# A gated recurrence and a multiplicative feed-forward on one core: the first 512 tokens handled by token halves, the last tile in two strips, and a new written order

## The chip, the cores and the metric

The kernel runs on one core of a Trainium2 chip. Its five engines work from queues of their own and meet at semaphores: TensorE (PE) multiplies matrices into PSUM, VectorE (DVE), ScalarE (ACT) and GpSimd (POOL) work elementwise, and SyncE (SP) issues the loads and stores, which the core's DMA engines carry out. The metric is the time of one execution on the device in microseconds (us); lower is better.

## The reference

There are 4 sequences of 5824 tokens with 256 channels, 23296 tokens in all. First comes a gated linear recurrence along each sequence, channel by channel:

```
log_a = 8 * sigmoid(r) * log(clip(sigmoid(a_param)))
a     = exp(log_a)
u     = sqrt(max(1 - a*a, 1e-6)) * sigmoid(i) * x
h[t]  = a[t] * h[t-1] + u[t]          # y = h
```

Then each token's y goes through a feed-forward with a product in place of an activation, with weights w1 and w2 (256 x 1024), w3 (1024 x 1024) and w_out (1024 x 256):

```
out = (((y @ w1) * (y @ w2)) @ w3) @ w_out
```

Inputs and output are float32.

## The kernel before

**Tiling.** Tokens go in chunks `c`: two of 256, then 44 of 512, then one of 256. The gates of chunks 0 and 1 are computed together, as one tile of 512 tokens that belongs to chunk 0 (`gates_of`). Each chunk passes through a line of steps, each with a letter in the written order:

- `r`, `i`, `x`: loads (L145). `R`: tanh of r (L157 where the tile is turned on PE, else L159). `V`: turn from tokens on partitions to channels on partitions, on PE against an identity (L197, for the chunks in `TURN_R`) or by a DMA (L208). `d`: the decay a = exp(scale * tanh + scale) (L220), one instruction for each half of 128 channels. `s`: its square (ACT L228, else L230). `q`: sqrt(1 - square) (L235).
- `I`: tanh of i (L165). `p`: plus one (L170, POOL). `t`: times x (L189 on POOL, two halves; L186 on DVE for chunk 0, with the plus one in it). `U`: the turn of this product u, on PE (L197, chunks in `TURN_U`) or by DMA.
- `g`: root times u (L245 or L248). `h`: the scan along time (L266), one for each channel half, starting from the chunk before. `y`: its cast to bf16 (L278).
- `a` and `b`: up products with w1 and w2 (L289). The 1024 hidden channels are four pairs of 128; `a` does one half pair into a PSUM tile of its own, `b` a whole pair. `c` copies `a`'s result to SBUF (ACT L305 or DVE L303, by the set `DV_COPY`). `m` multiplies the copy with `b`'s PSUM tile (L317, DVE).
- `D`: down product of 128 tokens (L331): 8 matmuls of 256 columns against a weight that is w3 @ w_out, folded once. `e` copies two such tiles out of PSUM, `o` stores them (L351). The last chunk has its own copies and stores, one for each 128 tokens (`evac_last`, `store_last`, L347).

**The fold.** The weights come in 512 KB pieces (`L..`), are cast to bf16 (`C..`: POOL L387, ACT L385 or DVE, by `W_ACT` and `W_DVE`), and each of w3's 8 row blocks is turned on PE (`Ft` L392), copied (`Fc`), multiplied with w_out (`Fm` L403) and scaled by 0.25 into the folded weight (`Fe`; ACT or DVE by `FOLD_ACT`). No `D` can run before the last `Fe`.

**Constants.** `A0` to `A2` compute the log-decay of each channel from `a_param` by a chain of tiny DVE instructions on 128x2 tiles.

**What sets the order.** The steps' order is written out as one string, `ORDER`, of 2457 words; each word emits its instructions, and every engine takes its own in that order and no other. `W` emits two matmuls on the identity whose result nobody reads. PSUM has two rings here: four buffers (`po`) shared by `a`, the turns, the fold and `D`, and two (`pb`) for `b` and `W`: the `b` two further on waits for the product `m` that reads the same buffer. Up to eight loads are under way at a time; the next is issued when an earlier one has landed.

Of the kernel before, what the change touches and what calls it, by code (L numbers as in the profile page):

```python
# [18 lines left out]
LOG1P = (2.00000001, 0.66666316, 0.40024854, 0.27961419, 0.28174657)  # L19
# [3 lines left out]
def kernel(  # L23
# [57 lines left out]
    TURN_U = {0, 2, 3, 4, 5, 6, 7}  # L81
# [3 lines left out]
    DV_SQUARE = {(0, 1), (11, 0)}  # L85
    AC_SQUARE = {(2, 0), (2, 1), (3, 0), (3, 1), (4, 0), (4, 1), (5, 0), (7, 0), (8, 0), (10, 0), (11, 1), (12, 0),
        (14, 0), (14, 1), (15, 0), (15, 1)}
    DV_CAST = set()
    AC_CAST = set()
    DV_COPY = {(0, 0, 0), (0, 0, 1), (0, 1, 0), (0, 1, 1), (0, 2, 0), (1, 0, 0), (1, 0, 1), (1, 1, 0), (1, 1, 1), (1,  # L90
        3, 0), (2, 0, 1), (2, 1, 0), (2, 1, 1), (2, 2, 0), (2, 3, 0), (2, 3, 1), (3, 0, 0), (3, 1, 0), (3, 2, 1), (3,
        3, 0), (4, 0, 0), (4, 0, 1), (4, 1, 1), (4, 2, 0), (4, 2, 1), (5, 1, 1), (5, 3, 0), (5, 3, 1), (6, 0, 0), (6,
        0, 1), (6, 2, 0), (6, 3, 1), (7, 0, 0), (7, 2, 0), (7, 3, 0), (7, 3, 1), (8, 3, 0), (10, 0, 1), (10, 1, 0),
        (10, 1, 1)}
    DV_EVAC = {(2, 0), (8, 0), (8, 1), (9, 0), (9, 1)}
    FOLD_ACT = {('c', 7), ('e', 3), ('e', 4)}
    W_ACT = {('w1', 1), ('w2', 0), ('w3', 0)}
    W_DVE = set()
# [3 lines left out]
    WARM = [2] * 16  # L102
    RINGS = {"r": 4, "i": 5, "x": 4, "th_r": 3, "u": 2, "rt": 2, "ut": 6, "a": 6, "nrm": 6, "h": 2, "y": 4,
# [38 lines left out]
    def load(c, nm):  # L142
        n = width(c) // P
        t = ring(loads, [P, 4, D], F32, name=nm + "_t", tag=nm)
        nc.sync.dma_start(  # L145
            out=t[:, :n, :],
            in_=src[nm][starts[c]:starts[c] + width(c), :].rearrange("(p n) c -> p n c" if long_rows(c) else "(n p) c -> p n c", p=P))
        T[nm, c] = t

    def tanh_r(c, half=None):  # L150
# [4 lines left out]
        if c in TURN_R:  # L155
            cols = slice(None) if half is None else slice(half * P, half * P + P)
            nc.scalar.activation(out=flat(t)[:, :n, cols], in_=T["r", c][:, :n, cols], func=AF.Tanh, scale=0.5)  # L157
        else:
            nc.scalar.activation(out=dense(t, n).rearrange("p cb j q -> p j cb q"), in_=cut(T["r", c])[:, :n],  # L159
                                 func=AF.Tanh, scale=0.5)  # L160
# [30 lines left out]
    def turn_pe(c, key, nm, half=None):  # L191
        n = width(c) // P
        cbs = range(NCB) if half is None else (half,)
        pt = ring(psum_o, [P, len(cbs), CT], BF16, name="ptr", tag="po")
        for cb in cbs:
            for j in range(n):
                nc.tensor.matmul(  # L197
                    out=pt[:, cb - cbs[0], j * P:(j + 1) * P],
                    lhsT=flat(T[nm, c])[:, j, cb * P:(cb + 1) * P], rhs=ident,
                    is_transpose=True,  # L200
                    start=(cb == cbs[0] and j == 0), stop=(cb == cbs[-1] and j == n - 1))
        T[(key, c) if half is None else (key, c, half)] = pt
# [9 lines left out]
    def decay(c, cb):  # L212
# [4 lines left out]
        pr = T["pr", c, cb][:, 0, :w] if ("pr", c, cb) in T else T["pr", c][:, cb, :w]  # L217
# [33 lines left out]
    def scan(c, cb):  # L251
        w = sizes[c]
        first = ("h", c) not in T
        if first:
            T["h", c] = ring(ypool, [P, NCB, CT], F32, name="h_t", tag="h")
        h = T["h", c][:, :, :w]
# [6 lines left out]
        if starts[c] % S != 0:  # L263
            pw = sizes[c - 1]
            init = T["h", c - 1][:, cb, pw - 1:pw]
        nc.vector.tensor_tensor_scan(h[:, cb, :], a[:, cb, :], n[:, cb, :], init, ALU.mult, ALU.add)  # L266

    def cast(c, cb=None):
        w = sizes[c]
        if ("y", c) not in T:  # L270
            T["y", c] = ring(ypool, [P, NCB, CT], BF16, name="y_t", tag="y")
        key = c if cb is None else (c, cb)
        cbs = slice(None) if cb is None else cb
        y, h = T["y", c][:, cbs, :w], T["h", c][:, cbs, :w]
# [11 lines left out]
    def up(c, m, dst, w_sb):  # L286
        w = sizes[c]
        for cb in range(NCB):
            nc.tensor.matmul(out=dst[:, :w], lhsT=w_sb[:, cb, m * P:(m + 1) * P],  # L289
                             rhs=T["y", c][:, cb, :w], start=(cb == 0), stop=(cb == NCB - 1))  # L290

    def up_a(c, mp, q):
        T["pa", c, mp, q] = pp = ring(psum_o, [P, CT], F32, name="pa", tag="po")
        up(c, 2 * mp + q, pp, w1_sb)

    def up_b(c, mp):
        T["pb", c, mp] = pp = ring(psum_b, [P, 2, CT], F32, name="pb", tag="pb")
        for q in range(2):
            up(c, 2 * mp + q, pp[:, q, :], w2_sb)
# [7 lines left out]
    def copy(c, mp, q):  # L307
        w = sizes[c]
        if ("sa", c, mp) not in T:
            T["sa", c, mp] = ring(ffn, [P, 2, CT], BF16, name="sa", tag="sa")  # L310
        copy_to((c, mp, q) in DV_COPY, T["sa", c, mp][:, q, :w], T["pa", c, mp, q][:, :w])

    def product(c, mp):
        w = sizes[c]
        if ("g", c) not in T:
            T["g", c] = ring(ffn, [P, KD, CT], BF16, name="g_t", tag="g")
        nc.vector.tensor_mul(out=T["g", c][:, 2 * mp:2 * mp + 2, :w], in0=T["sa", c, mp][:, :, :w],  # L317
                             in1=T["pb", c, mp][:, :, :w])

    def pair(c, j2):  # L320
        return min(2, sizes[c] // P - 2 * j2)

    def down(c, j):
        if c == NCH - 1:
# [309 lines left out]
```

## Time and profile before

The median of three executions is 511.82 us (511.63 to 512.12).

| | us |
|---|---|
| the profiled execution | 511.82 |
| its span, first to last instruction | 510.0 |
| PE busy | 502.2 (98%) |
| ACT busy | 463.3 (91%) |
| DVE busy | 429.8 (84%) |
| POOL busy | 318.2 (62%) |
| r of chunk 0 issued, landed | 0.74, 4.37 |
| first up product (chunk 0) | 13.30 |
| first up product of chunk 2 | 26.16 |
| last matmul group of the last chunk, copied out from | 506.90 |

A line of the profile names the line of the kernel, the engine, the operation and the tiles, written one first, with shapes; in the timeline the first two numbers are start and length, `xN` is how many instructions follow each other, and the bracket says how long the engine had stood and what released it. Lengths of neighbours on an engine overlap a little, so the distance between two starts tells better than a length what an instruction costs its queue. Matmuls are pipelined: a group of 128x512 matmuls starts one every 0.216 us, of 128x256 every 0.109 us, though each is shown longer.

### The profile page before, as it was taken

How to read it: one execution, taken by the hardware profiler on the slowest of the kernel's cores; microseconds unless marked ns; L12 is line 12 of the kernel's file. 1: busy time of each engine (PE TensorE's matmuls, PEld its weight loads, DVE VectorE, ACT ScalarE, POOL GpSimd, SP SyncE). 2: the span in 40 equal slices, each digit the busy share in tenths (PEclk: the TensorE clock that was granted, in tenths of full speed). 3: DMA queues.
4: the chain of work that ended last, by engine and by line, in shares of the span. 5: the costliest groups of instructions: out<-in, count | busy, mean ns of one | idle time of the engine just before them, and what ended most of it. 6: DMA issues, size and time to landing. Idle time of an engine off the chain costs nothing.

```text
span 510.0 us, 8879 instructions
## 1 busy us (share of the span) xinstructions
PE 502.2 (98%) x3217; PEld 308.2 (60%) x3217; DVE 429.8 (84%) x417; ACT 463.3 (91%) x711; POOL 318.2 (62%) x274
## 2 busy tenths in 40 slices
PE   7999999999999999999999999999999999999997
PEld 3777655665565656556666556565566655656566
DVE  5999999999999789878879799878877797959762
ACT  7999999998999999999999999998998979888543
POOL 3775878557558936965786973956647568580200
PEclk9999999999999999999999999999999999999999
DMA  8999999999989997896999996898786895252313
GB/s 319 407 413 307 379 275 276 304 302 257 309 232 282 303 282 248 191 322 184 256 306 317 262 285 163 233 245 227 206 250 151 231 319 149 91 164 64 66 48 105
DMA packets 177904, 124.06 MB, mean 243 GB/s; under 512 B 87362, under 2 KB 173892, under 8 KB 177860
## 3 DMA queue, kind: packets, MB, share of 16 engines
q1 hardware_dynamic: 177856, 123.50, 85.2%
q8 instruction: 25, 0.41, 0.3%
q14 instruction: 19, 0.16, 0.1%
q10 hardware_dynamic: 4, 0.00, 0.0%
HBM read 78.91 MB, written 23.86 MB: 201 GB/s over the span
## 4 chain that ended last, share of the span: by engine, by line
PE 90%; ACT 4%; DVE 2%; issue 2%; DMA 1%; DVEq 0%; ACTq 0%
PE po L331 30%; PE pb L289 29%; PE pa L289 28%; PE pw L403 1%; ACT sa L305 1%; PE ptr L197 1%; DVE g_t L317 1%; DMA r_t<-in_r_gate_dram 1%; PE ptw L392 1%; DVE sa L303 1%; DVE h_t L266 1%; ACT L165 1%; ACT L235 1%; ACT nrm L235 0%; ACT i_t L165 0%
## 5 line engine op out<-in xcount | busy, mean ns | idle before, releaser
L317 DVE TENSOR_TENSOR g_t<-sa,pb 128x1024 bf16<-128x1024 bf16 (+1 forms) x188 | 218.6, 1180 | 60.6 <-PE pb L289 29.0
L289 PEld LDWEIGHTS <-w_sb 128*128 128x128 bf16 x1504 | 146.5, 98 | 144.0 <-issue 3.4
L305 ACT CAST sa<-pa 128x512 bf16<-128x512 f32 (+1 forms) x336 | 180.9, 588 | 27.7 <-PE pa L289 17.6
L289 PE MATMUL pa<-y_t,w_sb 128*128 128x512 bf16 (+1 forms) x752 | 190.6, 372 | 0.4 <-ACT sa L305 0.2
L289 PE MATMUL pb<-y_t,w_sb 128*128 128x512 bf16 (+1 forms) x752 | 185.2, 372 | 0.6 <-DVE g_t L317 0.6
L331 PE MATMUL po<-wp_sb,g_t 128*128 128x256 bf16 x1456 | 178.0, 273 | 0.0
L331 PEld LDWEIGHTS <-g_t 128*128 128x128 bf16 x1456 | 142.4, 98 | 40.6 <-issue 0.5
L278 POOL CAST y_t<-h_t 128x1024 bf16<-128x1024 f32 (+2 forms) x49 | 52.5, 1074 | 146.0 <-DVE h_t L266 142.2
L189 POOL TENSOR_TENSOR u_t<-i_t,x_t 128x512 bf16<-128x512 f32 (+1 forms) x90 | 122.2, 1374 | 4.1 <-issue 2.0
L266 DVE TENSOR_TENSOR_SCAN h_t<-a_t,h_t,nrm 128x512 f32<-128x512 f32 (+1 forms) x92 | 120.8, 1343 | 1.6
L230 POOL TENSOR_TENSOR nrm<-a_t 128x512 f32<-128x512 f32 x74 | 83.0, 1139 | 12.9 <-ACT a_t L220 10.1
L220 ACT ACTIVATE a_t<-rt,la 128x512 f32<-128x512 bf16 (+1 forms) x82 | 66.0, 823 | 0.0
L305 ACT COPY ot<-po 128x512 f32<-128x512 f32 x86 | 50.5, 591 | 12.0 <-PE po L331 11.8
L248 DVE SCALAR_TENSOR_TENSOR nrm<-nrm,ut 128x1024 f32<-128x1024 f32 (+1 forms) x39 | 53.3, 1368 | 5.8 <-ACT nrm L235 5.8
L170 POOL TENSOR_SCALAR i_t<-i_t 128x1024 f32<-128x1024 f32 (+1 forms) x44 | 52.9, 1204 | 7.9 <-ACT i_t L165 7.9
L165 ACT ACTIVATE i_t<-i_t 128x1024 f32<-128x1024 f32 (+1 forms) x46 | 48.9, 1064 | 0.1
L235 ACT ACTIVATE nrm<-nrm 128x1024 f32<-128x1024 f32 (+1 forms) x47 | 48.3, 1041 | 0.2
L159 ACT ACTIVATE th_r<-r_t 128x1024 bf16<-128x1024 f32 (+1 forms) x41 | 43.5, 1060 | 0.0
L303 DVE CAST sa<-pa 128x512 bf16<-128x512 f32 (+1 forms) x40 | 23.4, 615 | 0.6 <-PE pa L289 0.5
L235 ACT ACT_TABLE_LOAD x17 | 21.8, 1283 | 0.3
L165 ACT ACT_TABLE_LOAD x9 | 11.5, 1283 | 0.2
L283 PE MATMUL warm<-ident 128*128 128x512 bf16 x32 | 10.1, 457 | 0.0
(55 smaller groups left out, 119.3 us busy)
## 6 DMA issues: line engine op xcount, KB each, us to landing
r_t<-in_r_gate_dram SPq DMA_DIRECT2D x45, 512.0 KB, 5.3
i_t<-in_i_gate_dram SPq DMA_DIRECT2D x45, 512.0 KB, 5.6
x_t<-in_x_dram SPq DMA_DIRECT2D x45, 512.0 KB, 5.5
out_dram<-ot SPq DMA_DIRECT2D x90, 256.0 KB, 3.3
wf<-in_moe_w_dram SPq DMA_DIRECT2D x12, 512.0 KB, 10.5
wf<-in_moe_w_out_dram SPq DMA_DIRECT2D x2, 512.0 KB, 10.6
rt<-th_r SPq DMA_TRANSPOSE x41, 4.4
ut<-u_t SPq DMA_TRANSPOSE x39, 4.1
```

The source lines that it names most:

```text
L165: nc.scalar.activation(out=t[:, :n, :], in_=t[:, :n, :], func=AF.Tanh, scale=0.5)
L170: (nc.vector if c in DV_PLUS else nc.gpsimd).tensor_scalar(t, t, 1.0, 1.0, op0=ALU.add, op1=ALU.mult)
L189: (nc.vector if (c, half) in DV_HALF else nc.gpsimd).tensor_mul(out=u, in0=t, in1=xt)
L220: nc.scalar.activation(out=a, in_=pr, func=AF.Exp, scale=la4[:, cb:cb + 1], bias=la4[:, cb:cb + 1])
L230: (nc.vector if (c, cb) in DV_SQUARE else nc.gpsimd).tensor_mul(out=n, in0=a, in1=a)
L235: nc.scalar.activation(out=n, in_=n, func=AF.Sqrt, scale=-1.0, bias=1.0)
L248: nc.vector.scalar_tensor_tensor(out=n, in0=n, scalar=1e-3, in1=T["pu", c][:, :, cols], op0=ALU.max, op1=ALU.mult)
L266: nc.vector.tensor_tensor_scan(h[:, cb, :], a[:, cb, :], n[:, cb, :], init, ALU.mult, ALU.add)
L289: nc.tensor.matmul(out=dst[:, :w], lhsT=w_sb[:, cb, m * P:(m + 1) * P], rhs=T["y", c][:, cb, :w], start=(cb == 0), stop=(cb == NCB - 1))
L305: nc.scalar.copy(out=dst, in_=src_ps)
L317: nc.vector.tensor_mul(out=T["g", c][:, 2 * mp:2 * mp + 2, :w], in0=T["sa", c, mp][:, :, :w], in1=T["pb", c, mp][:, :, :w])
L331: nc.tensor.matmul(out=po, lhsT=T["g", c][:, k, j * P:(j + 1) * P], rhs=wp_sb[:, k, :], start=(k == 0), stop=(k == KD - 1), skip_group_che ...
```

## The change

- r of chunk 0 (512 tokens) is loaded in two DMAs of 256 KB, each with half of the tokens; tanh and the turn on PE go by the same halves. Before, load and tile were whole, and tanh and turn went by channel halves. A decay instruction (128 channels, all 512 tokens) now reads both turned halves.
- For chunks 0 and 1 the first two of four pairs of up products are done on 256 tokens each, with both `a` halves in one PSUM tile, so that one copy serves both; the last two pairs are done once on 512 tokens. h, y and g of the two chunks share one tile, and the down product runs over them as one chunk.
- The down product of the last 128 tokens is done in two strips of 128 output channels, each with its copy (first DVE, then ACT) and its store.
- Chunk 9's u is turned on PE, no longer by a DMA.
- The chain of constants is one DVE instruction shorter.
- The sets that assign squares, casts, copies and evacuations to engines are new: six of `Fe` and `Fc` are on ACT, for three; of the weight casts ACT has two, for three, and DVE one; chunk 1's y is cast on DVE and ACT.
- The written order has 2442 words. It is new up to about chunk 14; its last 1607 words are those of before. In the new order w1's first piece is loaded ahead of i and x of chunk 0, and w3's piece 2 ahead of x of chunk 2. Of the 32 `W` matmuls, 4 stand ahead of the turns of r, 10 between them and the turn of u, 12 between that and the first up product, and 6 behind; before it was 4, 6, 16 and 6.

```diff
+LOG1P = tuple(c / 2 ** (2 * k + 1) for k, c in
+              enumerate((2.00000001, 0.66666316, 0.40024854, 0.27961419, 0.28174657)))
...
-    TURN_U = {0, 2, 3, 4, 5, 6, 7}
+    TURN_U = {0, 2, 3, 4, 5, 6, 7, 9}
...
-    FOLD_ACT = {('c', 7), ('e', 3), ('e', 4)}
-    W_ACT = {('w1', 1), ('w2', 0), ('w3', 0)}
-    W_DVE = set()
+    FOLD_ACT = {('c', 3), ('c', 7), ('e', 4), ('e', 5), ('e', 6), ('e', 7)}
+    W_ACT = {('w1', 1), ('w3', 0)}
+    W_DVE = {('w3', 5)}
...
+    HALVED = 2
...
-    def load(c, nm):
+    def load(c, nm, half=None):
         n = width(c) // P
+        js = slice(0, n) if half is None else slice(half * n // 2, (half + 1) * n // 2)
...
+        nc.sync.dma_start(out=T[nm, c][:, js, :], in_=rows[:, js, :])
...
-            cols = slice(None) if half is None else slice(half * P, half * P + P)
-            nc.scalar.activation(out=flat(t)[:, :n, cols], in_=T["r", c][:, :n, cols], func=AF.Tanh, scale=0.5)
+            js = slice(0, n) if half is None else slice(half * n // 2, (half + 1) * n // 2)
+            nc.scalar.activation(out=flat(t)[:, js, :], in_=T["r", c][:, js, :], func=AF.Tanh, scale=0.5)
...
+        js = range(n) if half is None else range(half * n // 2, (half + 1) * n // 2)
+        for cb in range(NCB):
+            for j in js:
...
+    def in_half(c, mp):
+        return c < 2 and mp < HALVED
+
+    def span(c, mp):
+        return part(c) if in_half(c, mp) else slice(0, width(c))
...
     def up_a(c, mp, q):
+        if in_half(c, mp):
+            if ("pa", c, mp) not in T:
+                T["pa", c, mp] = ring(psum_o, [P, 2, sizes[c]], F32, name="pa", tag="po")
+            up(c, mp, q, T["pa", c, mp][:, q, :], w1_sb)
+            return
...
+    def strips(c, j):
+        whole = not (c == NCH - 1 and j == sizes[c] // P - 1)
+        return [slice(0, D)] if whole else [slice(0, P), slice(P, D)]
...
     def store_last(c, j):
         t0 = starts[c] + j * P
-        nc.sync.dma_start(out=out[t0:t0 + P, :], in_=T["ot", c, j // 2][:, j % 2, :])
+        for cols in strips(c, j):
+            nc.sync.dma_start(out=out[t0:t0 + P, cols], in_=T["ot", c, j // 2][:, j % 2, cols])
...
     ORDER = """
-        r0 i0 x0 A3. E A0. A1. A2. R0.1 R0.0 W7 W10 V0.1 V0.0 W3 W14 W4 d0.1 s0.1 d0.0 s0.0 I0 q0.0 t0.0 t0.1 U0 g0
-        h0.0 W1 W2 W12 W5 W13 W8 W0 W15 h0.1 q0.1 g1 h1.1 h1.0 Lw1.0 Cw1.0 y0.1 y0.0 i2 Lw2.0 I2 r2 Lw1.1 Cw2.0 a0.0.1
...
+        r0.1 r0.0 Lw1.0 i0 x0 Lw2.0 i2 r2 Lw1.1 Lw3.2 x2 Lwo.1 Lwo.0 Lw2.1 r4 A3. E A0. A1. A2. R0.1 W6 W10 V0.1 R0.0
+        V0.0 d0.1 s0.1 d0.0 s0.0 I0 q0.0 t0.1 t0.0 W0 W14 W5 W3 W1 U0 W13 W12 W7 W15 W8 W9 g0 h0.0 h0.1 Cw1.0 Cw2.0
+        q0.1 I2 R2 y0.0 y0.1 a0.0.1 a0.0.0 W11 b0.0 V2 Cw3.2 g1 h1.0 h1.1 y1.0 Cw1.1 y1.1 d2.1 d2.0 s2.1 s2.0 q2 W2
+        a0.1.0 a1.0.1 a0.1.1 a1.0.0 c0.0.0 m0.0 b1.0 c1.0.0 m1.0 c0.1.0 a1.1.0 a1.1.1 W4 c1.1.0 b0.1 Ft2 Fc2 m0.1 p2
+        t2.0 t2.1 b1.1 U2 a0.2.0 a0.3.0 a0.2.1 Cwo.0 Cwo.1 Cw2.1 g2 m1.1 h2.0 h2.1 r3 R4 c0.2.0 c0.2.1 c0.3.0 R3
...
```

## The prediction

> **What bounds the kernel now.** I read the page's busy times first, then the chain that ended last, then the stretches, then the timeline of the first 30 us and of the last five.
>
> ```profile
> PE 502.2 (98%) x3217; PEld 308.2 (60%) x3217; DVE 429.8 (84%) x417; ACT 463.3 (91%) x711; POOL 318.2 (62%) x274
> PE 90%; ACT 4%; DVE 2%; issue 2%; DMA 1%; DVEq 0%; ACTq 0%
> ```
>
> PE is busy for 98% of the span and is 90% of the chain. The stretches tell where the rest is.
>
> ```profile
> 13.30:26.16 12.86, 12.47 (x119) 9.75 (x118) 12.74 (x25) 12.80 (x20) 9.68 (x11) 1.00 1.04 409
> 26.16:115.00 88.84, 88.79 (x628) 56.87 (x626) 85.94 (x98) 88.11 (x124) 61.87 (x56) 1.00 1.10 322
> 115.00:124.00 9.00, 8.42 (x48) 4.54 (x47) 8.70 (x9) 7.43 (x12) 7.42 (x5) 1.00 0.85 243
> 124.00:510.00 386.00, 382.59 (x2386) 232.94 (x2384) 314.78 (x264) 344.80 (x546) 235.16 (x194) 1.00 0.80 217
> ```
>
> The columns are length, then busy time of PE, PEld, DVE, ACT, POOL, then clock, DMA share, GB/s. From 26.16 to 115 us PE has 0.05 us without work, but ACT (0.73 us idle) and DVE (2.9 us) are nearly as full, and the DMA engines are saturated. So before 115 us four resources end together; after it PE alone. Any PE instruction added costs its full time, and only idle PE time can be won. There is little after 26.16: 0.58 us before one `pb` group at 122.8, and some tenths. The 1.5 us by which the first stretch exceeds its work (64 up matmuls of 0.109, 32 turns of 0.056, a fold of 0.44 and 0.87, 6 warm matmuls of 0.216: 11.3 us) is the rest of the prize, with the 13.3 us ahead of it.
>
> ```profile
> 4.40 1.15 ACT L157 ACTIVATE th_r<-r_t 128x512 bf16<-128x512 f32 x2 [1.33 <-DMA r_t<-in_r_gate_dram]
> 5.72 1.45 ACT L220 ACTIVATE a_t<-ptr,la 128x512 f32<-128x512 bf16 x2 [0.18 <-PE ptr L197]
> 7.07 1.05 ACT L165 ACTIVATE i_t<-i_t 128x1024 f32<-128x1024 f32 x1
> 9.43 1.15 ACT L235 ACTIVATE nrm<-nrm 128x512 f32<-128x512 f32 x2
> 10.11 0.75 DVE L245 SCALAR_TENSOR_TENSOR nrm<-nrm,ptr 128x256 f32<-128x256 f32 x2 [0.67 <-ACT nrm L235]
> 13.30 1.04 PE L289 MATMUL pa<-y_t,w_sb 128*128 128x256 bf16 x8
> 16.99 1.04 POOL L387 CAST w_t<-wf 128x1024 bf16<-128x1024 f32 x1
> 17.99 1.28 POOL L189 TENSOR_TENSOR u_t<-i_t,x_t 128x512 bf16<-128x512 f32 x1
> 25.07 1.04 POOL L278 CAST y_t<-h_t 128x1024 bf16<-128x1024 f32 x1 [2.85 <-DVE h_t L266]
> 26.16 1.02 PE L289 MATMUL pa<-y_t,w_sb 128*128 128x512 bf16 x4
> ```
>
> These are the head's links: tanh of r, decay, tanh of i, root, gating, first up product at 13.30; then the cast of chunk 2's y ends at 26.11 and chunk 2's up products start at 26.16. That second date carries my sum: by then all up products of chunks 0 and 1 are done, so whatever the head wins has to show as an earlier start of chunk 2.
>
> ```profile
> 506.43 1.21 SPq L347 DMA_DIRECT2D out_dram<-ot  x2
> 506.90 0.37 ACT L305 COPY ot<-po 128x256 f32<-128x256 f32 x1 [1.21 <-PE po L331]
> ```
>
> The tail: last copy out, last store issued at 507.30, landed 1.7 us later, span 510.0.
>
> **The head up to the first up product.** Loads land one after another: the first (r) 3.6 us after its issue at 0.74, the 4th at 8.7, the 7th at 12.5, the 9th at 15.4 (issued 4.74, 10.7 to landing), the 10th at 16.7, the 13th at 20.7, the 14th at 21.9. I keep these dates by rank, since the bytes are the same. Half of r is 256 KB: its landing lies between 2.2 us after the issue (the 1 KB of la_rows was used at 2.21) and the whole's 4.37; I take 3.7, nearer the whole, as the gap between queued loads is 1.3. The second half stays at 4.4. Tanh of half 1 (0.6) is then done by 4.4, of half 0 at 5.03. But decay now needs both turned halves; between tanh and decay the trace shows 0.69 (5.03 to 5.72). So decay starts at 5.72, as before: the 0.5 us saved on ACT becomes the wait for the turn, which the second tanh had covered. The weight w1.0 now goes ahead of i and x, so i lands third (6.9, or 7.4 if the weight takes the 1.8 that it took as 4th) and x fourth (8.2 to 8.7). Tanh of i starts at 7.07 to 7.45, the product with x (DVE, 2 x 0.69) at 8.2 to 8.8 against 8.15, gating at 10.1 to 10.5 against 10.11. POOL now casts the first y half while DVE scans the second, saving 0.36 of 12.86. The first up product follows at 12.7 to 13.2, where the 12 warm matmuls ahead of it (2.6 us after the turn of u) also end. First term: 0.1 to 0.6 us earlier.
>
> The Trainium skill, "SBUF — State Buffer", section "The DMA setup-cost knee", speaks against the split: each transfer pays some 2 us whatever its size. By its fit a half would land 2.6 us after issue, 3.3 and 3.8, and decay would start 0.5 us earlier, an estimate by that page; tanh of i would still wait for its load.
>
> **From there to chunk 2.** POOL's queue now is: cast w3.2, plus 2, two products t2, casts wo.0, wo.1, w2.1. The cast of w3.2 waits for the 9th load; before, x2 was 9th and POOL did plus 2 at 14.64. With starts 1.0 apart for casts and plus and 1.22 for products (16.99 to 17.99 to 19.21): w3.2 15.45, plus 16.45, t2 at 17.45 and 18.7, done 19.97; casts at 19.9, 20.9, 21.9, so w2.1 is ready at 22.9 (20.25 before). PE with the new order: its works from 13.0 (2 `a`, warm, `b`, turn, warm, 4 `a`, `b`, 2 `a`, warm, `b`, fold turn, `b`) reach the turn of u2 at about 19.4, after 0.7 us of waits for y1 (weight cast and y1.1 on ACT until 15.5) and for product 1.0 (DVE until 18.0). There it waits for t2, finishing the turn at 20.26; three `a` on 512 tokens (1.3) end at 21.55, the next `a` at 22.3, and `b0.2`, queued behind, waits for w2.1 until 22.95. Then b0.2, fold product, turn 4, b0.3 (0.86 + 0.87 + 0.44 + 0.86) end at 26.0, turn 3 at 26.45; tanh r3 on ACT has ended at 25.6 (r4 lands 14th, then tanh, three copies, tanh). y2 comes from gating at 20.5 (20.75 before) and so ends at 25.9. Chunk 2 starts at 26.45 with the same work behind it: 0.3 us later. Bounds: y2 and r3 leave at best 26.05 (-0.1), a load 0.7 us later puts it at 27.1 (+0.9).
>
> **What stays on PE.** Chunk 9's u moves from a DMA turn to PE: 8 matmuls of 0.056, +0.44, all on the path, as PE has no idle time there. The warm matmuls past the first up product are six in both. Merging the second pairs of chunks 0 and 1 leaves PE's columns as they were (32 matmuls of 0.109 for 16 of 0.216): 0.04 at most. DVE gets about 2.0 us more in all (six copies of 0.60 and a weight cast of 0.95 added, ten small copies of 0.33, two evacuations and folds taken), ACT 0.7 less, POOL 1.9 less; the removed DMA turn eases a full queue. Counting rows by order, ACT's work listed ahead of a PE step that needs it exceeded PE's own by up to 3.8 us before and by at most 2.7 in the new order; DVE's is behind PE's in both. That PE is no worse fed is thus likely: 0, between -0.9 (all idle after 26 us gone) and the DVE rival below.
>
> **Tail.** Two strips of 8 matmuls of 128 columns are 0.89 for 0.87. The last copy has 128 columns: between 0.37 (256) and 0.20 (2 columns); by the slope to 0.59 (512), 0.26. The first strip's copy and its store (0.34 on SP) are over when the last copy ends. The 64 KB store lands between 1.5 (la_rows, from its issue at 0.73 to its use at 2.21) and the 1.7 of 128 KB; I take 1.6. Sum -0.2, between 0 and -0.4. The constants' chain is one DVE step of 0.16 shorter and ends at 5.05, ahead of decay: nothing.
>
> **Sum.** The profiled execution took 511.82, which is the median; span 510.0 and 1.8 around it. +0.3 + 0.44 - 0.2 = +0.54: 512.4.
>
> **Rivals.** *DVE starves PE (slower).* Between 10 and 100 us DVE idles only 2.2 us, and it gets up to 2.0 us more. Where a product is late, the `b` two pairs on has no PSUM buffer and PE stands, as at 122.8. It decides once DVE is more than the 0.5 us behind that PE's buffers cover; then up to 2 us, with scans and copies behind it some more: 513 to 516. Against it: DVE's listed work stays behind PE's throughout. *The head's gain holds (still within 0.2%).* If DMA is quicker and w2.1 no wait, chunk 2 starts at 26.05 and the time is 511.9. *All idle goes (faster).* Best start, no stall after 26 us, tail -0.4: -0.1 + 0.44 - 0.9 - 0.4 = -1.0, 510.8; lower needs an error of mine in the head. *The order does something else:* loads of chunks 5 to 20 were reordered on a saturated queue; a late one stalls all: 514 and more.
>
> *The clock.* Warm matmuls start 0.43 us apart until 8.14, turns 0.06 apart from 9.50. Ten warm matmuls now stand ahead of the turn of u, six before; started at 5.5 at 0.43 each they end by 9.8, and u is ready at 9.6 to 10.1: nothing, or 0.2 us. The Trainium skill, "TensorE: Matmul & The Clock Gate", section "What's actually happening", lets the fast clock come after some 3.4 us of activity, in a window that runs free. By that page a window more at half speed could put the first up product back by up to 1.7 us, an estimate; the rows above agree with such a step but do not show when it comes in the new order.
>
> **How the numbers follow.** A run tells 0.2% (1.02 us) from no change. Fed PE with the head between its bounds: 0.58, all within 0.2% (511.2 to 512.8). DVE or load stalls: 0.33, over 0.2%. Faster by over 0.2%: 0.09. The range cuts a tenth at each end: 510.9 to 514.9, the upper end being DVE's 2 us on top of the sum and 0.5 for what hangs on it.
>
> **What would show it.** Decay of chunk 0 at 5.7; first up product at 12.7 to 13.2; PE idle before the turn of u2 and before b0.2, released by POOL; chunk 2's first 128x512 `pa` at 26.4; a turn of u9 on PE; last copy of 128 columns, 0.26. I am wrong if chunk 2 starts before 26.0, or if PE idles more than 1 us between 27 and 180.

## The result, and the profile after

The changed kernel takes 514.67 us (median of 7 executions, 513.35 to 515.96) against 511.90 (511.61 to 512.17) for the kernel before on the same chip: 1.0051 times as long, 95% interval 1.0038 to 1.0064. It is 0.5% slower, and that is more than the 0.2% that a run can tell. The profiled execution took 515.73 us, 1.06 above its median, with a span of 513.9; so the trace shows a loss of 3.9 us where the typical one is 2.8.

First the page of the kernel after: the busy times and the engines' shares of the chain that ended last.

```profile
PE 503.9 (98%) x3217; PEld 308.0 (60%) x3217; DVE 431.0 (84%) x413; ACT 462.7 (90%) x708; POOL 316.7 (62%) x271
PE 91%; ACT 3%; DVE 2%; DMA 2%; issue 1%; SPq 0%; DVEq 0%; ACTq 0%
```

Nothing in these totals explains 3.9 us: PE is busy 1.7 us longer, DVE 1.2, ACT and POOL less. The stretches say where the time is (length, then busy time of PE, PEld, DVE, ACT, POOL, then granted clock, DMA share, GB/s).

```profile
0.00:10.00 10.00, 6.18 (x23) 2.51 (x23) 3.71 (x16) 4.79 (x7) 1.74 (x7) 1.00 0.72 239
10.00:20.00 10.00, 7.94 (x41) 4.28 (x42) 6.74 (x13) 7.76 (x10) 5.07 (x6) 0.66 1.05 407
...
30.24:119.08 88.84, 88.69 (x633) 56.68 (x631) 86.84 (x99) 87.26 (x122) 60.10 (x54) 1.00 1.04 306
119.08:128.08 9.00, 8.96 (x59) 5.49 (x57) 8.87 (x9) 8.73 (x16) 5.83 (x5) 1.00 1.14 328
128.08:513.90 385.82, 382.56 (x2386) 232.49 (x2384) 315.75 (x265) 343.96 (x545) 238.14 (x194) 1.00 0.79 215
```

From 30.24 us on PE is as full as it was from 26.16 on before (0.15 us idle in 88.84, against 0.05), and in the stretch where 0.58 us was lost ahead of a `pb` group PE now misses 0.04. The rest of the kernel is no slower. What is new is in the first two rows: 239 GB/s in the first ten microseconds, and a granted clock of 0.66 in the second ten. The timeline of those links:

```profile
5.52 1.45 ACT L224 ACTIVATE a_t<-ptr,la 128x512 f32<-128x512 bf16 x2 [0.70 <-PE ptr L202]
8.14 1.04 POOL L417 CAST w_sb<-wf 128x1024 bf16<-128x1024 f32 x1 [6.84 <-DMA wf<-in_moe_w_dram]
9.39 1.06 ACT L169 ACTIVATE i_t<-i_t 128x1024 f32<-128x1024 f32 x1 [2.43 <-DMA i_t<-in_i_gate_dram]
10.71 1.29 DVE L190 SCALAR_TENSOR_TENSOR u_t<-i_t,x_t 128x512 bf16<-128x512 f32 x2 [3.02 <-DMA x_t<-in_x_dram]
12.06 1.03 PE L202 MATMUL ptr<-ident,u_t 128*128 128x128 bf16 x8 [3.48 <-DVE u_t L190]
12.89 5.03 PE L288 MATMUL warm<-ident 128*128 128x512 bf16 x12
17.76 0.60 PE L300 MATMUL pa<-y_t,w_sb 128*128 128x256 bf16 x4
30.24 1.45 PE L300 MATMUL pa<-y_t,w_sb 128*128 128x512 bf16 x6
```

Decay starts even earlier than before (5.52 for 5.72). Then three engines wait for loads: POOL for w1.0 until 8.14, ACT for i until 9.39, DVE for x until 10.71. PE stands 3.48 us before the turn of u, and the twelve warm matmuls behind it take 5.03 us, 0.42 each, where sixteen took 3.62 before. The first up product is at 17.76 (13.30 before). Chunk 2's first 128x512 `pa` is the group of six at 30.24 (earlier groups of that shape now belong to chunks 0 and 1): 4.08 us later than before, and the span is 3.9 us longer. Nearly all of the head's lateness reaches the end.

The DMA rates in steps of half a microsecond from 0 to 20 show the loss at its source, first the kernel before, then after. The row above each rate is the busy share of the core's DMA engines in the same steps, in tenths (9 is 90% or more):

```profile
DMA  0002949899999999999999999999999999999999
GB/s 0 0 0 100 287 172 377 352 442 352 385 418 397 336 328 307 410 410 402 410 430 422 418 389 401 426 344 397 442 418 393 397 410 397 381 387 385 379 426 408
```

```profile
DMA  0004789843996999999999999999999999999999
GB/s 0 0 0 109 287 328 320 131 86 111 209 197 225 344 369 393 401 422 430 418 414 397 410 442 438 385 414 406 410 430 442 412 379 391 408 375 385 391 393 420
```

Before, the rate stays above 300 from 3.0 us on. After, it falls to 131, 86 and 111 between 3.5 and 5.0 and is back above 340 only at 6.5. The fall begins between the landings of the two halves of r (3.30 and 4.17, by the trace), and w1.0, next in the queue, lands 3.9 us behind the second. Single packets of 2 KB, whose median is 0.08 us, take up to 1.5 there (the longest packet of the kernel before at the head takes 0.64). The engines' share sinks as well, to 0.8, 0.4 and 0.3 of the steps from 3.5 to 5.0, so for a part of that time engines have no packet at all, where before they are nearly full. The first 1.5 MB are in at 9.37 for 6.94, and since the queue stays full (a DMA share of 1.05 and 1.04 in the rows that cover 10 to 20 and 30 to 119 us), those 2.4 us of transfer are not made up for.

The tail is as it was meant: the last copy takes 0.27 and starts 3.0 us before the end of the span (3.1 before).

```profile
510.42 1.34 SPq L377 DMA_DIRECT2D out_dram<-ot  x3
510.90 0.27 ACT L323 COPY ot<-po 128x128 f32<-128x128 f32 x1 [1.23 <-PE po L358]
```

### The profile page after: what moved, and what is told of

The parts are those of the page before. It is cut to its first block, busy times and chain, and to the rows that moved or that the text cites. A ratio compares the mean times of both kernels' runs of the same rounds, so it can differ in the third digit from the quotient of the medians.

```text
span 513.9 us, 8864 instructions
## 1 busy us (share of the span) xinstructions
PE 503.9 (98%) x3217; PEld 308.0 (60%) x3217; DVE 431.0 (84%) x413; ACT 462.7 (90%) x708; POOL 316.7 (62%) x271
## 4 chain that ended last, share of the span: by engine, by line
PE 91%; ACT 3%; DVE 2%; DMA 2%; issue 1%; SPq 0%; DVEq 0%; ACTq 0%
PE po L358 30%; PE pa L300 28%; PE pb L300 28%; DMA x_t<-in_x_dram 2%; PE pw L437 1%; ACT sa L323 1%; PE warm L288 1%; PE ptr L202 1%; DVE g_t L338 1%; PE ptw L426 1%; ACT nrm L239 1%; ACT L239 0%; DVE h_t L271 0%; DVE sa L321 0%; ACT ot L323 0%
## 5 line engine op out<-in xcount | busy, mean ns | idle before, releaser
L300 PEld LDWEIGHTS <-w_sb 128*128 128x128 bf16 x1488 | 144.8, 98 | 148.0 <-issue 3.1
L323 ACT CAST sa<-pa 128x512 bf16<-128x512 f32 (+1 forms) x328 | 178.3, 595 | 28.4 <-PE pa L300 18.7
L358 PE MATMUL po<-wp_sb,g_t 128*128 128x256 bf16 (+1 forms) x1464 | 176.8, 272 | 0.0
L234 POOL TENSOR_TENSOR nrm<-a_t 128x512 f32<-128x512 f32 (+1 forms) x73 | 80.4, 1120 | 6.6 <-ACT a_t L224 4.5
L323 ACT COPY ot<-po 128x512 f32<-128x512 f32 (+1 forms) x87 | 51.0, 591 | 11.5 <-PE po L358 11.1
L321 DVE CAST sa<-pa 128x512 bf16<-128x512 f32 x40 | 26.6, 686 | 2.9 <-PE pa L300 2.2
L288 PE MATMUL warm<-ident 128*128 128x512 bf16 x32 | 12.0, 531 | 0.0
```

The costliest lines, as they stand in the source:

```text
L234: (nc.vector if (c, cb) in DV_SQUARE else nc.gpsimd).tensor_mul(out=n, in0=a, in1=a)
L300: nc.tensor.matmul(out=dst, lhsT=w_sb[:, cb, m * P:(m + 1) * P], rhs=T["y", gates_of(c)][:, cb, span(c, mp)], start=(cb == 0), stop=(cb == ...
L323: nc.scalar.copy(out=dst, in_=src_ps)
L358: nc.tensor.matmul(out=po, lhsT=T["g", c][:, k, j * P:(j + 1) * P], rhs=wp_sb[:, k, cols], start=(k == 0), stop=(k == KD - 1), skip_group_ ...
```

## The experiments

Two things stood to be told apart: whether the late loads come from the weight's place ahead of i and x or from r's halves, and what share the low clock has. Each run gives three dates that the others can be compared by: the landing of the first 1.5 MB of loads, the first up product, and chunk 2's start.

### The order of the loads, with the halves kept

```diff
-        r0.1 r0.0 Lw1.0 i0 x0 Lw2.0 i2 r2
+        r0.1 r0.0 i0 x0 Lw1.0 Lw2.0 i2 r2
```

> Undoes one move of the changed kernel: i and x of chunk 0 are loaded ahead of the first piece of w1, as in the kernel before. Theory A (the weight's late landing holds i and x back, and what follows from it is the loss): i lands at 5.6 to 5.9 us instead of 9.4, the first up product starts at 12.7 to 13.3 instead of 17.8, chunk 2's at 26.1 to 26.8 instead of 30.2, time 511.2 to 512.6. Theory B (the new order past the head costs: longer POOL queue, 2 us more on VectorE, one more turn on PE): the head shortens, but the time stays at 513.5 or more.

Measured: 513.72 us (12 executions, 513.19 to 514.88), 1.0022 times the kernel before (1.0008 to 1.0036). With i third, i still landed late: 6.46, which is 2.4 us behind the second half at 4.08 (before: 1.3 behind the whole r), and x at 8.00. The first up product came at 12.99, as early as I had predicted for the change, yet chunk 2 started at 27.96:

```profile
23.65 1.06 ACT L161 ACTIVATE th_r<-r_t 128x1024 bf16<-128x1024 f32 x1 [1.83 <-DMA r_t<-in_r_gate_dram]
25.23 1.03 PE L437 MATMUL pw<-wo_sb,w3t 128*128 128x256 bf16 x8 [0.85 <-ACT sa L323]
27.96 0.81 PE L300 MATMUL pa<-y_t,w_sb 128*128 128x512 bf16 x3
```

ACT waits for chunk 4's r until 23.65, the copies queued behind that tanh come late, and the fold's product waits for them. So the order accounts for part of the loss at most. Theory A, by which i would land at its old date once it stands ahead of the weight, is refuted: i is late behind the halves too. The time, 513.72, is in theory B's range, but by way of a late load and not of what B named.

### Another weight in w1.0's place

```diff
-        r0.1 r0.0 Lw1.0 i0 x0 Lw2.0 i2 r2 Lw1.1 Lw3.2 x2
+        r0.1 r0.0 Lw2.0 i0 x0 Lw1.0 i2 r2 Lw1.1 Lw3.2 x2
```

> The changed kernel with the first pieces of w1 and w2 exchanged in the load order: a piece of w2, of the same shape (rows of 2 KB out of 4 KB), goes ahead of i and x. If the shape or the place makes it late: i lands at 8.5 to 9.5. If it is w1 alone: i lands at 6.9 to 7.4.

```diff
-        r0.1 r0.0 Lw1.0 i0 x0 Lw2.0 i2 r2 Lw1.1 Lw3.2 x2
+        r0.1 r0.0 Lw3.2 i0 x0 Lw1.0 Lw2.0 i2 r2 Lw1.1 x2
```

> The changed kernel with a piece of w3 (512 KB in one run, rows of 4 KB) loaded in the place ahead of i and x, and w1's first piece after x. If the place makes a load late, whatever it is: i lands at 8.5 to 9.5. If it is the 2 KB rows of w1: i lands at 6.9 to 7.2 and the slow stretch of the load queue comes after x, as in the kernel before.

Measured, one execution each: 512.76 us with w2.0 there, 516.23 with w3.2. The load behind the halves landed at 7.15 and at 8.00, x at 9.61 and 10.53, chunk 2 started at 27.22 and 30.46. w3.2 comes in whole rows of 4 KB, w1.0 in pieces of 2 KB; so neither the tensor nor the length of the weight's rows is the cause. Whatever stands behind the halves is late, by amounts that differ. The two times differ by more than the landings do (0.9 us), so they say little about which weight stands there.

### The clock, by itself

```diff
-    WARM = [2] * 16
+    WARM = [2, 18] + [2] * 14
```

> The changed kernel with 16 more warm matmuls ahead of the turn of u, where PE stands idle for 3.5 us; the loads stay as they are. Theory A1 (the idle PE falls back to the slow clock, and the 12 warm matmuls after it at 0.43 us each hold up the first up product): the matmuls after the turn start 0.216 apart, the first up product comes at 15.7 to 16.0 instead of 17.8, chunk 2 at 28.3 to 29, time 1.2 to 2 us less, 512.7 to 513.5. Theory A2 (chunk 2's start hangs on the late loads alone): first up product earlier, chunk 2 still at 30, time 514.3 to 515.

Sixteen more warm matmuls fill the wait ahead of the turn of u. Measured: 513.78 us (12 executions), 1.0021 times before (1.0006 to 1.0036). The row of the second ten microseconds:

```profile
10.00:20.00 10.00, 9.21 (x67) 5.61 (x66) 8.34 (x16) 9.93 (x14) 5.32 (x6) 1.00 1.05 408
```

The clock stays at 1.00. The loads are as late as in the changed kernel (w1.0 7.83, x 10.36), the turn of u stands at 11.81, but from there to the first up product (14.86) it takes 3.05 us and not 5.70, and chunk 2 starts at 28.86 and not at 30.24. So theory A1 came in its dates (the first up product even earlier than it said), with a time 0.3 us above its range. Between these two executions the low clock is worth at most 1.4 us at chunk 2, as 0.25 of it is there already at the turn of u, where x was in earlier; what remains of the 4.1 is there with the clock kept up. The other executions agree on the clock: over the span it was 0.999 or 1.000 in all twelve of this kernel, and 0.993 to 0.997 in all seven of the changed one.

### r in one load, the rest of the change kept

```diff
-        r0.1 r0.0 Lw1.0 i0 x0 Lw2.0
+        r0 Lw1.0 i0 x0 Lw2.0
```

> The changed kernel in its own order (w1.0 ahead of i and x) with r in one DMA. Theory H: w1.0 lands at 5.7 to 6.3, i at 7.0 to 7.6, x at 8.2 to 8.9 (with halves 8.09, 9.37 and 10.61); the turn of u starts at 9.6 to 10.2, the first up product at 12.7 to 13.5, chunk 2's at 26.2 to 27.3; 512.0 to 513.2. Theory W: w1.0 lands at 7.5 or later, i after 8.8, chunk 2 starts at 29.5 to 30.5, 514 to 515.5.

One execution: 511.90 us. The same kernel was then timed:

> The changed kernel with r of the first 512 tokens in one DMA and nothing else undone, now timed against the kernel before. Theory H (the two half loads are the loss): as in its first execution, w1.0 lands at 5.8 to 6.3, chunk 2 starts at 26.1 to 27.0, and the time is 511.6 to 512.7, within 0.2% of before. Rival W (the weight's place, or the rest of the change, has a share of its own that one execution did not show): 513.2 or more, over 0.2% slower.

Measured: 512.32 us (12 executions, 511.80 to 512.82), 0.9999 times the kernel before (0.9987 to 1.0011). The whole of the 0.5% is gone with one edit. By the medians, taken relative to the kernel before, 0.22% of it (1.1 us) is there with the halves and the clock kept up (1.0021, with the sixteen more warm matmuls), and the other 0.30% (1.5 us) is the clock's; by the medians in microseconds (512.32, 513.78, 514.67) it is 1.5 and 0.9. The sizes of the two shares are no surer than that. Its DMA rates, and its timeline from tanh of r to chunk 2:

```profile
GB/s 0 0 0 76 164 270 381 344 348 340 430 418 410 393 393 393 410 418 442 418 393 434 434 373 410 356 373 430 451 410 375 383 379 383 385 391 410 399 447 401
```

```profile
4.30 1.15 ACT L161 ACTIVATE th_r<-r_t 128x512 bf16<-128x512 f32 x2 [1.29 <-DMA r_t<-in_r_gate_dram]
6.15 1.45 ACT L224 ACTIVATE a_t<-ptr,la 128x512 f32<-128x512 bf16 x2 [0.70 <-PE ptr L202]
8.58 1.29 DVE L190 SCALAR_TENSOR_TENSOR u_t<-i_t,x_t 128x512 bf16<-128x512 f32 x2 [0.25 <-ACT i_t L169]
9.93 0.62 PE L202 MATMUL ptr<-ident,u_t 128*128 128x128 bf16 x8 [0.39 <-DVE u_t L190]
12.98 0.70 PE L300 MATMUL pa<-y_t,w_sb 128*128 128x256 bf16 x4
19.98 0.51 PE L202 MATMUL ptr<-ident,u_t 128*128 128x128 bf16 x6 [0.50 <-POOL u_t L193]
22.93 1.04 PE L300 MATMUL pb<-y_t,w_sb 128*128 128x512 bf16 x4 [0.39 <-POOL w_sb L417]
26.44 1.46 PE L300 MATMUL pa<-y_t,w_sb 128*128 128x512 bf16 x6
```

The rate no longer falls. w1.0 lands at 5.81, i at 7.10, x at 8.38, PE waits 0.39 and not 3.48 us before the turn of u, and the clock holds. This is the head that the prediction described, down to the two waits of PE for POOL; only decay is later (6.15 for 5.72).

Then both edits together, whole r with i and x first:

```diff
-        r0.1 r0.0 Lw1.0 i0 x0 Lw2.0
+        r0 i0 x0 Lw1.0 Lw2.0
```

> The changed kernel with r of the first 512 tokens loaded in one DMA, followed by i and x and only then w1.0 (tanh and turn still go by token halves). Theory H (halves): it is the two 256 KB loads that make the next load land 2.3 to 3.9 us behind them, whatever that load is. Then i lands at 5.6 to 5.8 and x at 6.9 to 7.1 as before the change (6.46 and 8.00 with halves in this order), decay of chunk 0 starts at about 5.7, the first up product at 12.3 to 13.3, chunk 2's at 26.0 to 27.0 (27.96 with halves), and the time is 511.2 to 512.6. Theory W (the weight): the late landing comes with the weight's place alone, the whole load changes nothing against the same order with halves; chunk 2 starts at 27.5 to 28.3, 513.3 to 514.2.

Measured: 512.65 us (12 executions), 1.0006 times before (0.9991 to 1.0021). i lands at 5.53 and x at 6.77, and still chunk 2 starts at 26.95, later than with w1.0 ahead (26.44). The lines of the two engines that work there, DVE's two products with x and POOL's two casts:

```profile
8.56 2.14 DVE L190 SCALAR_TENSOR_TENSOR u_t<-i_t,x_t 128x512 bf16<-128x512 f32 x2 [0.26 <-ACT i_t L169]
8.78 2.83 POOL L417 CAST w_sb<-wf 128x1024 bf16<-128x1024 f32 x2 [7.47 <-DMA wf<-in_moe_w_dram]
```

Two products take 2.14 us for 1.29, two casts 2.83 for 2.08 (2 x 1.04). In the trace the second product takes 1.53 where it takes 0.68 with no cast beside it. With w1.0 loaded ahead, its cast is over (5.87 to 6.91) before the products begin at 8.58.

### The halves in the kernel before, and the weight in the kernel before

```diff
-        nc.sync.dma_start(
-            out=t[:, :n, :],
-            in_=src[nm][starts[c]:starts[c] + width(c), :].rearrange(...))
+        rows = src[nm][starts[c]:starts[c] + width(c), :].rearrange(...)
+        for js in [slice(2, 4), slice(0, 2)] if (nm, c) == ("r", 0) else [slice(0, n)]:
+            nc.sync.dma_start(out=t[:, js, :], in_=rows[:, js, :])
```

> The kernel before with only this edit: r of the first 512 tokens in two DMAs, second half of the tokens first; tanh, turn and order are its own. Theory H: i, the next load, lands at 6.2 to 6.8 (5.68 before), x at 7.7 to 8.3 (6.94), tanh of i starts at 7.1 as before, the product with x waits for x until about 8.2, and the head is later by 0 to 0.6 us with a gap of 2 us or more between the second half's landing and i's: 511.8 to 512.6. Theory W: i at 5.4 to 5.8 and x at 6.7 to 7.1, the time that of before within 0.2 us.

Measured: 513.54 us (12 executions, 512.70 to 515.73), 1.0024 times before (1.0008 to 1.0041). The split alone makes the kernel before slower, by more than I had allowed it. Its DMA rates, then its timeline and its second ten microseconds:

```profile
GB/s 0 0 0 80 197 410 348 98 139 123 106 303 385 385 365 360 344 332 348 373 418 414 401 434 406 422 414 401 414 426 438 401 410 406 426 391 381 389 381 403
```

```profile
7.97 1.06 ACT L165 ACTIVATE i_t<-i_t 128x1024 f32<-128x1024 f32 x1 [1.16 <-DMA i_t<-in_i_gate_dram]
9.35 1.29 DVE L186 SCALAR_TENSOR_TENSOR u_t<-i_t,x_t 128x512 bf16<-128x512 f32 x2 [2.48 <-DMA x_t<-in_x_dram]
11.04 5.30 PE L283 MATMUL warm<-ident 128*128 128x512 bf16 x16
16.18 1.04 PE L289 MATMUL pa<-y_t,w_sb 128*128 128x256 bf16 x8
```

```profile
10.00:20.00 10.00, 9.57 (x62) 5.76 (x63) 7.78 (x18) 8.55 (x11) 6.87 (x9) 0.83 1.05 409
```

The fall of the rate is there, at the same place, with i as the next load: the halves landed at 3.32 and 3.95, i only at 7.95, 4.0 us later. Both theories had i earlier: H is right in kind and short by over a microsecond. The clock falls too, to 0.83 over the stretch: eight of the sixteen warm matmuls start 0.43 apart. It does not fall in all executions: over the span it was 0.993 to 0.997 in four of the twelve, and 0.999 or 1.000 in eight.

```diff
-        r0 i0 x0 A3. E
+        r0 Lw1.0 i0 x0 A3. E
...
-        h0.0 W1 W2 W12 W5 W13 W8 W0 W15 h0.1 q0.1 g1 h1.1 h1.0 Lw1.0 Cw1.0
+        h0.0 W1 W2 W12 W5 W13 W8 W0 W15 h0.1 q0.1 g1 h1.1 h1.0 Cw1.0
```

> The kernel before with w1.0 loaded right behind the whole r, ahead of i and x. Theory H: w1.0 at 5.7 to 6.3, i at 7.0 to 7.6, x at 8.2 to 8.9; i and x are each 1.3 us or so later than in the kernel before, tanh of i starts with the landing at 7.1 to 7.6, the product with x at 8.3 to 8.9, so the first up product is 0 to 0.8 us later (13.3 to 14.1) and the time 511.8 to 512.7. Theory W: w1.0 at 7.5 or later, the first up product at 15 or later, 513.5 to 515.

Measured, one execution: 514.83 us. The loads did what theory H said (w1.0 6.02, i 7.32, x 8.56), so the weight's place does not make it land late. The time did not: the first up product came at 16.48, not at 13.3 to 14.1. POOL's cast ran beside DVE's products (the second took 1.52 for 0.68), the turn of u ended at 11.34, and then the clock fell: sixteen warm matmuls took 5.30 us. The constants, too, were 1.05 late in this execution, and decay stood 0.82 us for them. What I had left out of that expectation were these three, not a load.

### What of the split costs

```diff
+        for ps in [slice(64, P), slice(0, 64)] if (nm, c) == ("r", 0) else [slice(0, P)]:
+            nc.sync.dma_start(out=t[ps, :n, :], in_=rows[ps, :, :])
```

> The kernel before with r of the first 512 tokens in two DMAs of 256 KB that split it by partitions (64 each), so that every row is the 4 KB it was in one DMA. Theory S (two small loads at the head of the queue are the cause, whatever their rows): i lands at 7.0 or later (7.95 with the split by token halves), x at 8.3 or later. Theory R (the rows of 2 KB are the cause): i lands at 5.4 to 6.0 and x at 6.7 to 7.3, as with the whole r (5.68 and 6.94). 511.7 to 512.4 by R, 512.5 to 515 by S.

```diff
+        for js in [slice(2, 4), slice(0, 2)] if (nm, c) == ("i", 0) else [slice(0, n)]:
+            nc.sync.dma_start(out=t[:, js, :], in_=rows[:, js, :])
```

> The kernel before with r whole and the second load, i of the first 512 tokens, in two DMAs by token halves. Theory P (the collapse comes only where the halves stand at the head of the queue, while the DMA engines start up): the halves of i land at 5.0 to 5.2 and 5.6 to 5.9, x at 6.8 to 7.3, and the time is that of before within 0.3 us. Theory A (halves stall the load behind them wherever they stand): x lands at 8.5 or later, the product with x waits for it, 512.5 to 515.

Measured, one execution each: 513.16 us with r split by partitions, 512.36 with i split by tokens. Both fell between their two theories by their landings; by the times, 513.16 is in the range of S, and 512.36 is as long as the kernel before was beside it (512.37 in the median), as P has it. The rates, first r by partitions, then i by tokens:

```profile
GB/s 0 0 0 2 131 295 279 262 221 98 401 426 393 397 389 389 348 311 336 389 418 406 426 422 401 414 406 414 426 418 418 401 422 401 385 403 383 387 385 385
```

```profile
GB/s 0 0 0 133 33 344 418 250 234 336 246 176 291 434 381 385 406 426 418 418 393 401 459 401 406 401 410 455 418 401 410 459 365 397 404 385 381 391 383 387
```

With rows of 4 KB (by partitions) the rate still sinks, to 98 at 4.5 us, the second half of r lands at 5.35 (4.37 whole) and x at 8.22 (6.94); chunk 2 starts 1.4 us late (27.53 for 26.16). With i split, i is in only at 6.57 (5.68) and x at 7.98; the product with x starts at 8.11, as before, but the later loads keep the lag and chunk 2 starts at 26.80, 0.6 late. So neither the 2 KB rows nor the place at the head of the queue is needed for a late load, by these two executions, though the latest landings are where both come together. Over all fourteen profiled executions the landing of the first 1.5 MB separates the two kinds without overlap:

| loads at the head | executions | first 1.5 MB landed, us |
|---|---|---|
| r, i and the next weight or x each in one DMA | 6 | 6.77 to 7.32 |
| r or i in two DMAs | 8 | 7.98 to 9.37 |

The second row is 1.0 to 2.4 us more than the kernel before (6.94). Why the packets slow down and the DMA engines stand isn't shown by these runs, nor why the size differs. The table does not say that a head can only be late by a split: two of the six in its first row started chunk 2 at 29.24 and 29.84, from a late start of the constants, a POOL cast beside DVE's products and a low clock, with their loads on time. And of 64 executions of the kernel before that were timed beside these runs, ten took 513.5 to 515.9 us, six of them at a clock of 0.997 or less; none of the ten was profiled.

### Chunk 9's turn, back on DMA

```diff
-        r0.1 r0.0 Lw1.0 i0 x0 Lw2.0
+        r0 Lw1.0 i0 x0 Lw2.0
...
-    TURN_U = {0, 2, 3, 4, 5, 6, 7, 9}
+    TURN_U = {0, 2, 3, 4, 5, 6, 7}
```

> The changed kernel with r in one DMA and chunk 9's u turned by a DMA again, not on PE. If PE's added work lies on the path as the prediction has it, the time is 0.44 us less than with r in one DMA alone (511.3 to 512.2), and PE has 8 turns fewer. If the DMA turn comes late and PE waits for it, or loads behind it are delayed, the 0.44 is given back: 511.8 or more, with an idle of PE before the gating of chunk 9 is read.

Measured: 514.75 us (7 executions, 514.45 to 517.31), 1.0053 times before (1.0032 to 1.0074): 2.4 us above the version with the turn on PE (512.32). In the profiled execution, a long one (517.31), the head was late too, though its loads were not (i in at 6.99): the constants started 1.05 late, a POOL cast ran beside DVE's products, and the clock was 0.83 between 10 and 20 us. But from chunk 2's start to the last copy it took 482.65 us, against 480.70 with the turn on PE, and that is 1.95 us that the head has no part in. The place in this kernel's timeline, then the stretch of ten microseconds around it in this kernel, then the same stretch with the turn on PE:

```profile
103.07 2.29 DVE L252 SCALAR_TENSOR_TENSOR nrm<-nrm,ut 128x1024 f32<-128x1024 f32 x1 [0.80 <-DMA ut<-u_t]
107.38 0.59 PE L300 MATMUL pa<-y_t,w_sb 128*128 128x512 bf16 x2 [0.82 <-DVE sa L321]
109.68 1.02 PE L300 MATMUL pb<-y_t,w_sb 128*128 128x512 bf16 x4 [0.41 <-DVE g_t L338]
```

```profile
100.00:110.00 10.00, 8.51 (x55) 5.08 (x53) 9.09 (x9) 9.17 (x15) 3.66 (x4) 1.00 0.94 269
```

```profile
100.00:110.00 10.00, 10.00 (x59) 5.49 (x57) 9.60 (x11) 9.97 (x16) 6.70 (x7) 1.00 1.04 302
```

Chunk 9's turn was issued at 97.57 and landed at 102.88. DVE's gating stands 0.80 us for it until 103.07 and then takes 2.29 itself, beside a POOL product that starts at 103.00, where chunk 8's took 1.21; the copies and products queued behind it on DVE come late, and PE misses 1.49 us in these ten. So in this order the DMA turn is 2 us dearer than the turn on PE. That does not say that a DMA turn costs 2 us: the new order is written for a turn on PE, with 9 words between `U9` and `g9`, where the order of before has 60. There the DMA turn was issued at 93.57, and the gating at 99.53 did not wait for it. The changed kernel with whole r and a `U9` placed earlier, on DMA, was not run.

## Why the prediction was right or wrong

The time, 514.67, lies inside the range (510.9 to 514.9), and the likeliest case, within 0.2%, did not come: slower by 0.5%, which had a chance of 0.33. That the range holds it is luck: its upper end was DVE's 2 us and 0.5 for what hangs on it, and DVE did not hold PE up.

**The step that failed** is in the head's paragraph: "I keep these dates by rank, since the bytes are the same". The halves themselves landed as costed or earlier (3.30 and 4.17, for 3.7 and 4.4), but the step priced a split by its own landing alone and left every later rank where it was. Measured: i at 9.37 for 6.9 to 7.4, x at 10.61 for 8.2 to 8.7. The rank dates held where r came whole in this order: i at 7.10 and 7.17, x at 8.38 and 8.43. The term "0.1 to 0.6 us earlier" for the first up product became 4.5 later in the profiled execution, and with r whole it was 0.2 to 0.3 earlier. Two slips in the prediction's working did no harm: the "2.2 us after the issue" of la_rows is a date (2.21, 1.5 after its issue), and the works listed for the first stretch add up to 11.4 us, not 11.3.

**The page on the transfer's fixed cost.** By the fit that the prediction took from the Trainium skill, "SBUF — State Buffer", section "The DMA setup-cost knee", the halves were to land at 3.3 and 3.8; the trace has 3.30 and 4.17, and 3.32 and 3.95 in the kernel before with the split. The fit comes within 0.4 us on the halves. What decided the time is what happened to the load behind them, and for that the prediction had no term, from the rows or from the page.

**The clock.** The prediction allowed "nothing, or 0.2 us" from the rows, and named 1.7 us at most by the page "TensorE: Matmul & The Clock Gate". The granted clock was 0.66 over ten microseconds, and filling the wait was worth up to 1.4 us at chunk 2 (2.65 at the first up product: 5.70 less 3.05). It did not come from the ten warm matmuls ahead of the turn, which the paragraph argued about, but from the 3.48 us without work behind them, since filling those kept the clock up. That page, in the section "What's actually happening", has a window that runs free of the kernel; the runs agree that the length of a wait alone does not fix it: with 2.96 us of idle at that place (w2.0 second) the clock held at 1.00, with 1.69 (the kernel before with halves) it fell to 0.83.

The traces show more. At the head the warm matmuls go from 0.43 to 0.216 us apart at a moment that differs between executions (5.9 to 11.5; 6.15 and 8.54 in two of one kernel, the one with r whole), and in all four executions in which the clock fell, it fell 3.41 us after that moment and came back one such step later, or two in the changed kernel (so that the 2.65 us at the first up product are more than the estimate of 1.7, which was for one). So I read PE's busy time by these steps, first the changed kernel from 7.25 on, then w2.0 second from 6.53:

```profile
7.25:10.66 3.41, 1.33 (x6) 0.39 (x4) 0.44 (x1) 1.25 (x2) 1.04 (x1) 1.00 1.03 413
10.66:14.07 3.41, 2.01 (x11) 1.29 (x12) 2.16 (x5) 3.38 (x4) 1.04 (x1) 0.50 1.03 415
```

```profile
6.53:9.94 3.41, 1.57 (x7) 0.49 (x5) 1.16 (x3) 1.71 (x3) 0.00 (x0) 1.00 1.04 418
9.94:13.35 3.41, 2.29 (x17) 1.34 (x18) 2.62 (x5) 3.37 (x5) 2.02 (x2) 1.00 1.03 413
```

In the four executions PE was busy for 1.33 to 1.49 us of the step ahead of the fall, that is idle for 1.92 to 2.08; in the ten where the clock held, it was never idle for more than 1.84 of a step, by the profile. The 2.96 us of w2.0 second lay across two steps, 1.84 and 1.12. In these runs, then, it is the idle inside one step that decides, and where the steps lie the kernel does not choose.

**From there to chunk 2** the prediction's chain can be read where its head came true, in the version with r whole. Predicted: turn of u2 waiting for POOL and done at 20.26; b0.2 waiting for w2.1 until 22.95; y2 at 25.9; chunk 2 at 26.45. Measured there: 0.50 us of wait for POOL and the turn done at about 20.4, b0.2 at 22.93 after 0.39 for POOL's cast, y2's cast ending at 26.2, chunk 2 at 26.44 and 26.23. In the changed kernel itself, with everything 4 us later, b0.2 no longer waits for POOL.

**What stays on PE.** From chunk 2's start to the last copy the sum had +0.46 (0.44 for the turn, 0.02 for the strips); measured 480.66 for 480.74, so -0.08. The turn's 0.44 is there, and the 0.58 us of idle ahead of `pb` that stood at 122.8 is gone. "No worse fed: 0" was too careful by half a microsecond, inside its bound of -0.9. The turn on PE is not what took that wait away: with the turn back on DMA the wait ahead of `pb` does not come back at that place (96.7 us after chunk 2's start), and what PE loses in that version it loses 71 to 84 us after that start. So the price of the turn holds for its own work, and which change of the order removed the wait isn't shown.

**The tail**: 0.26 predicted for the last copy, 0.27 measured; the whole step -0.1 for -0.2. The constants ended at 4.99, not on the path in the changed kernel; in three of the fourteen profiled executions the first of them started 1.05 later, and there decay waited for them in two.

**The rivals.** DVE did not starve PE: busy 1.2 us more, and PE's idle past chunk 2 fell. "The head's gain holds" did not come even with r whole: its time did in one execution (511.9), but not its reason, as chunk 2 started at 26.23 and 26.44 after a wait for w2.1, which is the main sum's case. The rival that came was the last, "a late load stalls all: 514 and more", in kind and in size; but I had looked for it among the reordered loads of chunks 5 to 20, and it was the third load of the kernel. Of the two signs of error, chunk 2 before 26.0 and PE idle between 27 and 180, neither appeared; a third, chunk 2 long after 26.4, should have been named. Of what was to show the prediction right, the first up product (17.76), chunk 2's start (30.24) and the two waits of PE for POOL failed in the changed kernel.

The sum, remade from dates that were measured: 511.82; head with r whole +0.3 (26.44 for 26.16, as predicted); loads behind the halves +2.4 (28.86 with the clock kept up, for 26.44); clock +1.4 (30.24 for 28.86); PE from chunk 2 to the last copy -0.1; tail -0.1. That is 515.7, the profiled execution's 515.73; the first three terms are distances between dates of single executions, so they add up by construction, and by the medians above the second and third are nearer to each other. The prediction had the first, fourth and fifth of these terms to within 0.6 us and lacked the two in the middle.

No version here beats the kernel before beyond what a run can tell. The change without its split is level with it.

## What to carry to other kernels

At the head of a kernel whose DMA queue is full from the start, don't price a split load by its own earlier landing: look at the rate and the landing of the load behind it, since what that loses was carried here by the loads behind it as long as the queue was full. The rank-by-rank table of landings held here where the transfers kept their size, and only there. And when PE stands at the head for about 2 us, add the clock to its price: here the low clock behind the wait cost more than half of what the late loads did in the profiled executions (1.4 beside 2.4), and about as much by the medians.

## What the runs showed of the hardware that I had not expected

- With the first 512 KB load cut into two of 256 KB by tokens, the load behind them landed 2.4 to 4.0 us after the second; behind the whole one the next landed 1.3 to 1.6 us after it. The DMA rate fell from above 300 to a lowest step of 57 to 258 GB/s in the six executions, for one to three microseconds, with single packets at up to 1.6 us. The size varies between executions that begin alike: i, right behind the same halves, landed at 6.46 in one and at 7.95 in another.
- A POOL cast of 128x1024 beside a DVE product of two SBUF tiles made them take turns: product 1.53 for 0.68, casts 1.38 and 1.50 for 1.04. In the kernel before the cast alone paid (1.55, products 0.69 and 0.68). One load moved so that the cast came earlier took the collision away; chunk 2 was at 26.44 for 26.95, though other loads moved with it.
- The granted clock fell below 1.00 between 10 and 20 us in four of the fourteen profiled executions, to 0.83 in three and 0.66 in one. In two of the three it was eight warm matmuls 0.43 apart, 3.4 us in all, and then full speed again. PE had stood 1.2 to 3.5 us just ahead; in another execution it stood 2.96 there and the clock held. What told the two apart was the idle inside one step of 3.41 us, counted from the clock's rise: 1.92 us and more, or 1.84 and less.
